# The first microseconds rearranged: tap diagonals on VectorE, a shorter first convolution on TensorE, and w_in loaded in three pieces

## The chip, the cores and the metric

The kernel runs on one core of a Trainium2 chip. The metric is device time in microseconds, from the launch to the end of the program. Four runs of the kernel before gave a median of 681.24 us, between 681.12 and 681.43. One execution was profiled; it took 681.22 us, of which the trace's span, from the first recorded instruction to the last, holds 679.5 us. The remaining 1.7 us lie around the span.

## What is computed

A lightweight causal convolution over tokens, 7 taps wide, with one softmaxed set of taps for each of 8 heads (24 channels a head, 192 in all), followed by a two-layer network with a leaky ReLU. There are 8 sequences of 4096 tokens, so 32768 rows in all.

```python
# x: (8, 4096, 192)   weight: (8, 7)
w = softmax(weight, axis=-1)                       # one row of taps a head
x_pad = concatenate([zeros(6 tokens), x], axis=1)
conv[b, s, h, g] = sum_k w[h, k] * x_pad[b, s + k, h, g]
# w_in: (192, 2048)   w_out: (2048, 192)
h = conv.reshape(32768, 192) @ w_in
out = maximum(0.01 * h, h) @ w_out                 # float32
```

## The kernel before

**Tiling.** Channels lie in three chunks (`NCH`) of 64 (`CH`). Two sequences share the 128 partitions: the tile `xt[:, c, token]` has chunk c of sequence 0 on partitions 0 to 63 and of sequence 1 on 64 to 127. Work goes by `groups`: the first two blocks of 512 tokens are cut into four half groups of 256 tokens, and 30 whole groups of 512 follow. For each group TensorE forms the first product (`mm1`, line 494, into `ph`), ScalarE applies the leaky ReLU to `g` (line 501), and TensorE forms the second product of the group before (lines 511 and 574, into `po` and `acc2`). VectorE convolves the next group's tokens, one instruction for each tap and chunk (lines 226 and 232), and transposes the result (line 596); SyncE stores it (line 612). Order on each engine is the order of the program text; tiles carry their own waits. SyncE's queue also issues the DMA transposes of x (lines 117 and 203), and GpSimd's queue issues all loads.

**The start.** The first group has no group before it under which VectorE could convolve, so TensorE convolves it: a diagonal matrix of 64 x 64 holds one tap of 64 channels, and matrix products with shifted windows of `xt` add up in PSUM. A tap is split into a bf16 high part and a low part (`p` = 0 and 1), so a chunk needs 2 x 7 diagonals, each used on both 64-row halves. The array runs as four tiles of 64 x 64. `pe_conv_jobs` makes a list of pairs of matmuls, one pair for each diagonal; a chunk with `cross=True` sends its output to the other half of the columns, so that a straight and a crossed list together use all four tiles. `run` interleaves lists. The program text calls a slot of such a list a place: up to four matmuls of 256 columns that use different tiles at the same time. Before, the order is 7 places of chunk 0 alone, 7 of chunk 0 with chunk 2, 7 of chunk 1 with chunk 2 and 7 of chunk 1 alone: 28 places, 84 matmuls.

The diagonals are products of a folded identity (`ident2`, 128 x 64, bf16) with the taps (`whm`, float32, copied out of PSUM at line 407). VectorE makes five of these tables with `diag_wide` (line 413), ScalarE the other ten single diagonals with `diag_each` (line 421). After its diagonals VectorE forms `wml`, `rsum` and its reciprocal, then copies the first piece of w_in into the layout that the row tiles need (`spread_down`, line 320, and `spread_up`, line 323), takes one half of chunk 2 out of PSUM (line 276), copies the transposed x of the second half group (line 199) and forms `wk`, the float32 taps for its own convolutions. ScalarE takes the other accumulators out (line 452).

w_in comes in two pieces of 8 blocks of 128 columns (`load_w_in`, line 314). GpSimd's queue issues: piece 0 (two loads), x of half group 1 (`x_rows`, line 148, two loads), piece 1 (two loads), x of half group 2 (two), w_out (line 346, two), x of half group 3 (`x_half`, line 152, six), then x of block 2 (line 99). A unit `u` of `mm1` for a half group takes two blocks of w_in; units 0 to 3 use piece 0, units 4 to 7 piece 1. Between the units of the first group TensorE convolves chunks 0 and 2 of the second half group in the cuts `CUTS` = 6, 5 and 3 places, while VectorE convolves its chunk 1 and spreads piece 1.

**The stores.** `evac_t` stores a group with four DMAs (line 612); one group, number 17 of 34, is stored in eight smaller ones.

## Time and profile before

| what | value | how to read it |
|---|---|---|
| median of four runs | 681.24 us | 681.12 to 681.43 |
| the profiled execution | 681.22 us | its span is 679.5 us |
| TensorE matmuls, weight loads | 99%, 66% of the span | ends of matmuls are modelled, so this is occupancy and not peak rate |
| VectorE, ScalarE, GpSimd | 71%, 76%, 22% | busy share of the span |
| first matmul of the convolution (line 257) | at 5.60 us | 28 places follow |
| first transpose of half group 1 (line 188) | at 8.79 us | 12 matmuls |
| first matmul of the first product (line 494) | at 9.25 us | 24 matmuls, units 0 and 1 |
| first leaky ReLU (line 501) | at 10.13 us | |
| group 17's eight stores (line 612) | issued from 356.78 us, 5.58 us in all | other groups: four stores, 2.80 us |
| bytes moved | 53.27 MB, mean 78 GB/s | DMA engines are busiest in the first 16 us |

Times are microseconds from the start of the span. PE is TensorE's matmul, PEld its weight loads, DVE is VectorE, ACT ScalarE, POOL GpSimd and SP SyncE; L494 is line 494. In a timeline row the columns are start, length, engine, line, operation, tiles, shape and count.

### The profile page before, as it was taken

The page shows a single profiled execution, that of the slowest core. Times are in us where ns is not written, and L with a number is a line of the kernel's source. Part 1 is how long each engine was busy: PE and PEld are TensorE (multiplying, and loading weights), DVE is VectorE, ACT ScalarE, POOL GpSimd, SP SyncE. Part 2 cuts the span into 40 slices and gives each one's busy share as a digit, 9 for nine tenths or more (in the row PEclk, how much of TensorE's full clock was granted, in tenths as well). Part 3 has the DMA queues.
Part 4 walks back from the last instruction along what each step waited for, and adds up shares of the span by engine and source line. Part 5 has one row for each costly group of instructions (what it writes and reads, how often), then busy time and mean ns, then how long its engine had stood idle before and what let it go on. Part 6 is the DMA issues. An engine that isn't in the chain of part 4 may idle for free.

```text
span 679.5 us, 27093 instructions
## 1 busy us (share of the span) xinstructions
PE 675.7 (99%) x12444; PEld 447.4 (66%) x12444; DVE 480.6 (71%) x811; ACT 518.8 (76%) x608; POOL 146.3 (22%) x205
## 2 busy tenths in 40 slices
PE   9999999999999999999999999999999999999998
PEld 6997666666666666666666666666666666666667
DVE  7989467766768666778667687667786676876612
ACT  7899777777777778777777877778777777777781
POOL 7455210222201222211222112222022220000000
PEclk9999999999999999999999999999999999999999
DMA  9899846656647657556556565567465573321123
GB/s 152 97 115 104 55 79 88 80 64 72 91 75 96 73 55 88 83 85 86 63 65 89 82 92 73 59 84 94 73 87 68 61 96 71 72 56 33 34 49 94
DMA packets 213890, 53.27 MB, mean 78 GB/s; under 512 B 209296, under 2 KB 213392, under 8 KB 213776
## 3 DMA queue, kind: packets, MB, share of 16 engines
q0 software_dynamic: 98752, 13.97, 30.3%
q1 hardware_dynamic: 115008, 37.57, 27.5%
q8 instruction: 97, 1.59, 1.0%
q14 instruction: 17, 0.14, 0.1%
q10 hardware_dynamic: 16, 0.00, 0.0%
HBM read 28.31 MB, written 25.17 MB: 79 GB/s over the span
## 4 chain that ended last, share of the span: by engine, by line
PE 99%; DVE 0%; issue 0%
PE ph L494 49%; PE acc L574 44%; PE po L511 5%; PE acc L257 1%; PE warm L358 1%; PE ptr L188 0%; PE ptr L179 0%; DVE o_sb L624 0%; PE warm L394 0%; PE wps L394 0%
## 5 line engine op out<-in xcount | busy, mean ns | idle before, releaser
L501 ACT ACTIVATE g<-ph 128x1024 bf16<-128x1024 f32 x512 | 496.6, 1021 | 140.2 <-PE ph L494 140.0
L232 DVE SCALAR_TENSOR_TENSOR yt<-xt,wk,yt 128x512 bf16<-128x512 bf16 (+1 forms) x582 | 380.6, 719 | 0.2
L494 PE MATMUL ph<-yt,w_in 64*64 64x512 bf16 (+2 forms) x6048 | 377.1, 369 | 0.0
L574 PE MATMUL acc<-g,w_out 64*64 64x512 bf16 x5568 | 339.9, 376 | 0.0
L494 PEld LDWEIGHTS <-w_in 64*64 64x64 bf16 (+1 forms) x6048 | 229.5, 131 | 102.9 <-issue 0.6
L574 PEld LDWEIGHTS <-w_out 64*64 64x64 bf16 x5568 | 178.6, 118 | 118.5
L99 POOL DMA_DIRECT2D x_bf<-in_x_dram x180 | 133.9, 775 | 408.8 <-DMA xt<-x_bf 406.7
L596 DVE STREAM_TRANSPOSE o_t<-acc 128x512 f32<-128x512 f32 x87 | 72.1, 866 | 182.7 <-PE acc L574 182.7
L511 PE MATMUL po<-w_out,g 64*128 64x192 bf16 (+1 forms) x640 | 36.8, 243 | 0.0
L511 PEld LDWEIGHTS <-g 64*128 64x128 bf16 (+1 forms) x640 | 32.5, 95 | 3.2 <-issue 0.4
L226 DVE TENSOR_SCALAR yt<-xt,wk 128x512 bf16<-128x512 bf16 (+1 forms) x97 | 29.1, 325 | 2.9 <-ACT g L501 2.2
L584 ACT COPY junk<-junk 128x1 f32<-128x1 f32 x58 | 11.2, 192 | 4.1
L624 DVE COPY o_sb<-po 128x192 f32<-128x192 f32 x8 | 2.8, 356 | 6.8 <-PE po L511 4.2
L257 PE MATMUL acc<-xt,diag 64*64 64x256 bf16 x140 | 5.4, 272 | 0.0
L624 ACT COPY o_sb<-po 128x192 f32<-128x192 f32 x16 | 5.1, 324 | 0.3
L257 PEld LDWEIGHTS <-diag 64*64 64x64 bf16 x140 | 4.3, 106 | 1.3 <-DVE diag L413 0.7
L358 PE MATMUL warm<-const-bfloat16-1.0 128*128 128x512 bf16 (+3 forms) x12 | 4.3, 513 | 0.8 <-PEq L736 0.8
L152 POOL DMA_DIRECT2D x_half<-in_x_dram x6 | 4.3, 732 | 1.2 <-DMA x_rows<-in_x_dram 0.9
L358 PEld LDWEIGHTS <-const-bfloat16-1.0 128*128 128x128 bf16 x12 | 1.5, 138 | 2.5 <-issue 2.5
L148 POOL DMA_DIRECT2D x_rows<-in_x_dram x4 | 2.9, 742 | 0.0
L413 DVE TENSOR_TENSOR diag<-ident,whm 128x448 bf16<-128x448 bf16 (+1 forms) x5 | 2.6, 579 | 0.0
L421 ACT ACTIVATE diag<-ident,whm 128x64 bf16<-128x64 bf16 x10 | 2.5, 339 | 0.0
(47 smaller groups left out, 24.4 us busy)
## 6 DMA issues: line engine op xcount, KB each, us to landing
out_dram<-o_t SPq DMA_DIRECT2D x112, 192.0 KB, 4.7
x_bf<-in_x_dram POOLq DMA_DIRECT2D x180, 64.0 KB, 3.1
out_dram<-o_sb SPq DMA_DIRECT2D x8, 192.0 KB, 3.4
xt<-x_bf SPq DMA_TRANSPOSE x90, 3.7
w_out<-in_moe_w_out_dram POOLq DMA_DIRECT2D x2, 384.0 KB, 8.2
out_dram<-o_t SPq DMA_DIRECT2D x8, 96.0 KB, 2.1
out_dram<-o_sb SPq DMA_DIRECT2D x8, 96.0 KB, 1.7
w_in<-in_moe_w_in_dram POOLq DMA_DIRECT2D x2, 256.0 KB, 4.7
```

Source lines behind the costliest of these rows:

```text
L99: ins = nc.gpsimd.dma_start(out=t[:, c, :, e, :], in_=src[2 * rp + e, :, :, c * CH : (c + 1) * CH],)
L226: lambda s=src, d=dst, c=c: nc.vector.tensor_scalar_mul(d, s, wk[:, c, 0:1])
L232: lambda s=src, d=dst, c=c, k=k: nc.vector.scalar_tensor_tensor(out=d, in0=s, scalar=wk[:, c, k : k + 1], in1=d, op0=mybir.AluOpType.mult, ...
L257: lambda k=k, p=p, a=a, ps=ps, to=to, acc=accs[e * apart]: nc.tensor.matmul(out=acc[to, :T], lhsT=diag[c][ps, p, k, :], rhs=xt[0][ps, c, a ...
L358: nc.tensor.matmul(out=wa[:, 0, 0:cols], lhsT=ones[:, 0:128], rhs=ones[:, 0:cols], start=True, stop=True,)
L494: nc.tensor.matmul(out=ph[m : m + M, e, i * T : (i + 1) * T], lhsT=w_in_of(f, e, c, m, m + M), rhs=y[ps, c, t0 : t0 + T], start=(c == chun ...
L501: act = nc.scalar.activation(out=g[blk][:, nf * u : nf * (u + 1), :, t0 : t0 + T], in_=ph.rearrange("p e (i t) -> p i e t", i=nf), func=my ...
L511: return nc.tensor.matmul(out=po[m], lhsT=g[b][ps, fc, e, s * 128 : (s + 1) * 128], rhs=w_out[ps, fc, :], start=start, stop=stop,)
L574: ins = nc.tensor.matmul(out=acc2[gi, r][e * CH : (e + 1) * CH, 0:T], lhsT=w_out_of(ps, fc, r), rhs=g[b][ps, fc, e, t0 : t0 + T], start=fi ...
L584: seal = nc.scalar.copy(out=junk, in_=junk)
L596: nc.vector.transpose(out=osb[gi, 0][:, 0 : T // GB, :, r], in_=acc2.pop((gi, r))[:, 0:T].rearrange("p (j k) -> p j k", k=GB),)
L624: ins = copy(out=o_sb[:, n % 2, :], in_=po.pop(n))
```

## The change

1. The taps are copied out of PSUM as bf16 with every tap twice (`taps`), and each table of diagonals is one VectorE product over pairs of elements. All six tables are made on VectorE; ScalarE's ten single diagonals go. `wml`, `rsum`, its reciprocal and `wk` stand between and behind the tables.
2. The first convolution runs chunks 0 and 2 together through 14 places. Chunk 1 then uses all four array tiles by itself: its 256 tokens are cut in halves of 128, a straight and a crossed one (`pe_conv_quads`), in 14 slots of four matmuls with 128 columns, which the text counts as 7 places. The crossed half accumulates in the PSUM tile `wps`, and three instructions take chunk 1 out in place of one.
3. w_in comes in three pieces of 4, 4 and 8 blocks, the second and third between x of half groups 1 and 2. The second is spread right after the copies of half group 1, the third after two of VectorE's taps in place of three.
4. The first unit of `mm1` runs chunk by chunk over both of its blocks, in place of block by block.
5. Group 17 is stored in four DMAs like the others.

```diff
-    def diag_wide(c, p, n):
-        nc.vector.tensor_mul(
-            diag[c][:, p, 0:n],
-            ident2[:, None, :].to_broadcast([128, n, CH]),
-            whm[:, c, p, 0:n, None].to_broadcast([128, n, CH]),
-        )
-
-    def diag_each(c, p, ks):
-        for k in ks:
-            nc.scalar.activation(
-                out=diag[c][:, p, k, :], in_=ident2,
-                func=mybir.ActivationFunctionType.Copy, scale=whm[:, c, p, k : k + 1],
-            )
+    taps = const_pool.tile([128, NCH, 2, K + 1, 2], BF16, name="taps")
+    nc.vector.tensor_copy(
+        out=taps, in_=wps_hm[..., None].to_broadcast([128, NCH, 2, K + 1, 2])
+    )
+    def diag_wide(c, p):
+        shape = [128, K, CH // 2, 2]
+        nc.vector.tensor_mul(
+            diag[c][:, p].rearrange("p k (m t) -> p k m t", t=2),
+            ident2.rearrange("p (m t) -> p m t", t=2)[:, None].to_broadcast(shape),
+            taps[:, c, p, 0:K, None, :].to_broadcast(shape),
+        )
...
+    def pe_conv_quads(grp, c, crossed):
+        blk, t0, T = grp
+        n = T // 2
+        acc = psum_o.tile([128, ST], FP32, name="acc", tag="po")
+        accs = [(acc, acc), (crossed[:, 0], crossed[:, 1])]
+        jobs = []
+        for p in range(2):
+            for k in range(K):
+                a = BASE + k + blk * ST + t0
+                four = []
+                for h in range(2):
+                    for e in range(2):
+                        ps = slice(e * CH, (e + 1) * CH)
+                        to = slice((e ^ h) * CH, ((e ^ h) + 1) * CH)
+                        four.append(
+                            lambda k=k, p=p, a=a + h * n, ps=ps, to=to, acc=accs[h][e]: nc.tensor.matmul(
+                                out=acc[to, :n], lhsT=diag[c][ps, p, k, :],
+                                rhs=xt[0][ps, c, a : a + n],
+                                start=(k == 0 and p == 0),
+                                stop=(k == K - 1 and p == 1),
+                            )
+                        )
+                jobs.append(four)
+        def evac(straight, *scale):
+            y = yt[blk][:, c, t0 : t0 + T]
+            straight(y[:, 0:n], acc[:, :n], rsum[:, c, :])
+            for e in range(2):
+                ps = slice(e * CH, (e + 1) * CH)
+                frm = slice((1 - e) * CH, (2 - e) * CH)
+                scale[e](y[ps, n:T], crossed[frm, e, :n], rsum[frm, c, :])
...
-    NPW = 2
+    PIECES = [(0, RUN), (RUN, 2 * RUN), (2 * RUN, NFC)]
...
-    for rows in (0, 128):
-        load_w_in(1, rows)
+    for n in range(1, len(PIECES)):
+        for rows in (0, 128):
+            load_w_in(n, rows)
     load_first(2)
...
-    for p in range(2):
-        diag_wide(0, p, K)
-    diag_wide(2, 0, K)
-    diag_wide(1, 1, VK)
-    diag_wide(2, 1, K)
-    diag_each(1, 1, range(VK, K))
-    diag_each(1, 0, range(K))
+    diag_wide(0, 0)
+    diag_wide(2, 0)
+    diag_wide(0, 1)
+    nc.vector.tensor_add(wml, wps_l, taps[:, :, 1, :, 0])
+    diag_wide(2, 1)
...
+    diag_wide(1, 0)
     nc.vector.reciprocal(rsum, rsum)
+    diag_wide(1, 1)
...
-    pe_1, evac_1 = pe_conv_jobs(groups[0], 1, (1, 0))
-    run(pe_0[:K])
-    run(pe_0[K:], pe_2[:K])
+    pe_1, evac_1 = pe_conv_quads(groups[0], 1, wps)
+    run(pe_0, pe_2)
     evac_0(act_scale)
-    run(pe_1[:K], pe_2[K:])
-    run(pe_1[K:])
-    evac_2(act_scale, nc.vector.tensor_scalar_mul)
-    evac_1(act_scale)
+    evac_2(nc.vector.tensor_scalar_mul, act_scale)
+    run(pe_1)
+    evac_1(act_scale, nc.vector.tensor_scalar_mul, act_scale)
     transpose_first(1)
     evac_first(1, nc.vector.tensor_copy, nc.vector.tensor_copy)
...
+    spread_down(1)
+    spread_up(1)
...
-        for n in range(nf * NCH):
-            i, c = n // NCH, chunks[n % NCH]
+        wide = not (blk or t0 or u)
+        order = [(i, c) for i in range(nf) for c in chunks]
+        if wide:
+            order = [(i, c) for c in chunks for i in range(nf)]
+        for i, c in order:
...
-            parts = 2 if gi == len(groups) // 2 else 1
-            for h, q in product(range(2), range(parts)):
+            for h in range(2):
...
-                    for job in conv_1[:3]:
+                    for job in conv_1[:2]:
                         job()
-                    spread_down(1)
-                    spread_up(1)
-                    for job in conv_1[3:]:
+                    spread_down(2)
+                    spread_up(2)
+                    for job in conv_1[2:]:
```

## The prediction

> **What bounds the kernel now.** I read the page's first part and the chain that ended last, then the same chain over the first 20 us.
>
> ```profile
> span 679.5 us, 27093 instructions
> ...
> PE 675.7 (99%) x12444; PEld 447.4 (66%) x12444; DVE 480.6 (71%) x811; ACT 518.8 (76%) x608; POOL 146.3 (22%) x205
> ...
> PE 99%; DVE 0%; issue 0%
> ```
>
> TensorE is the chain from end to end. Is any of it waiting? ScalarE's marker between two rounds (line 584) comes once at the same point of each whole group; the timeline around the middle has it at:
>
> ```profile
> 341.82 0.19 ACT L584 COPY junk<-junk 128x1 f32<-128x1 f32 x1
> ...
> 362.54 0.19 ACT L584 COPY junk<-junk 128x1 f32<-128x1 f32 x1
> ...
> 403.98 0.19 ACT L584 COPY junk<-junk 128x1 f32<-128x1 f32 x1
> ...
> 424.70 0.19 ACT L584 COPY junk<-junk 128x1 f32<-128x1 f32 x1
> ```
>
> That is 20.72 us a group (403.98 - 362.54 is twice that). A group has 384 matmuls, and the chain lists 24 of them in 1.29 us, 54 ns each: 384 x 54 ns = 20.7 us. Nothing stalls there, so only the start can give or take time. The chain there, as start, length, engine, tile:
>
> ```profile
> 5.67 3.19 PE acc L257 x80
> 8.86 0.46 PE ptr L188 x12
> 9.31 1.43 PE ph L494 x24
> 10.75 0.78 PE acc L257 x24
> ...
> 12.97 0.67 PE acc L257 x20
> 13.64 1.55 PE ph L494 x24
> 15.19 0.45 PE acc L257 x12
> ```
>
> The reader sees TensorE work without a gap from 5.67 us. From 0.78 us for 24 matmuls and 0.45 us for 12, three places of four cost 0.33 us, 0.11 us a place, and each change of shape about 0.12 us. Then 28 places should take 28 x 0.11 + 0.12 = 3.20 us; they take 3.19. So the diagonals do not hold the convolution up even now: an earlier diagonal gives nothing by itself, and only fewer places do.
>
> **Place count (part 2 of the change).** Chunks 0 and 2 take 14 places: 14 x 0.11 = 1.54 us. Chunk 1 takes 14 slots of four matmuls with 128 columns. No row has four tiles at 128 columns. These are the nearest:
>
> ```profile
> 6.50 0.13 PEld L257 LDWEIGHTS <-diag 64*64 64x64 bf16 x4
> ...
> 8.79 0.53 PE L188 MATMUL ptr<-ident,x_rows 128*64 128x128 bf16 x12
> ```
>
> The first is a 10 ns look at the weight loads: four of them, each 106 ns long (the tile's row gives 102/106/108), all lie inside 0.13 us. So the four tiles are loaded at the same time and their issue takes about 25 ns for four. The second is a run with 128 columns and two tiles: 0.46 us in the chain, less 0.12 for the change of shape, is 0.34 us for six pairs, 56 ns a pair, so one tile takes a new weight and 128 columns every 56 ns. If four tiles do what two do, a slot costs 56 ns and chunk 1 14 x 0.056 = 0.78 us. That is the low end. The high end is one matmul at a time at the smallest mean spacing in the trace, 0.34 us / 12 = 28 ns: 56 x 28 = 1.57 us. I take 0.78, by the weight-load row, which has this very tile shape. The convolution then takes 1.54 + 0.78 + 0.12 = 2.44 in place of 3.19: 0.75 us less; at the high end 0.04 more.
>
> The Trainium skill speaks against this part. "TensorE: Matmul & The Clock Gate", section "Wait — 56ns, not 53.3ns?", says that the starts of successive matmuls are never closer than about 25 ns, however few columns they have. By that figure, as an estimate, chunk 1 would take 56 x 25 ns = 1.4 us and the part would give 0.1 us. The page does not say whether it holds across array tiles, and the four loads above inside 0.13 us say that it need not.
>
> **Diagonals (part 1).** They remove ten ScalarE instructions (339 ns each, 2.49 us together, 5.33 to 7.82) and the five tables on VectorE. The rows of the stretch 4.4 to 9.9 us, grouped by shape:
>
> ```profile
> L413 DVE TENSOR_TENSOR diag<-ident,whm 128x448 bf16<-128x448 bf16 x4 | 2.3, 620 | 0.0
> ...
> L413 DVE TENSOR_TENSOR diag<-ident,whm 128x256 bf16<-128x256 bf16 x1 | 0.4, 418 | 0.0
> ```
>
> Slope (620 - 418) / 192 = 1.05 ns an element, fixed part 149 ns. Successive tables start 0.54 us apart (five in 2.56 us), 0.08 less than their length. The new table has bf16 on both sides in adjacent pairs. The nearest row of that kind is the sum of two bf16 halves of the identity (line 383): 64 elements in 174 ns, where 149 + 64 x 1.05 would be 216 and half the slope 183. So I take half the slope: 149 + 448 x 0.525 = 384 ns, 0.30 apart. The bounds are that and 620 ns, 0.54 apart. With VectorE starting at 4.47 (the copy of 96 in place of 48 elements adds 0.05), the tables end at 4.85 (0,0), 5.16 (2,0), 5.46 (0,1), 5.96 (2,1), 6.46 (1,0) and 6.96 (1,1), with 0.2 us for each small step between. TensorE needs them at 5.60, 5.60, 6.40, 6.40, 7.17 and 7.56: covered by at least 0.4 us, so they cost nothing.
>
> "VectorE: DVE Perf Modes", section "The perf-mode tier table (the rule you actually need)", gives a two-input product on bf16 twice the float32 rate; an estimate from that rule, half of 448 x 1.05 ns, makes a table 0.23 us shorter.
>
> **What then decides the first product (parts 2 and 4).** VectorE goes on: `wk` (0.20 + 0.20, moved here from behind the transposes), the spread of piece 0 at half its size (rows 423 and 824 ns for 1024 and 2048 elements, so 0.22 and 0.42) ending at 7.95, its half of chunk 2 (461 ns, line 276) ending at 8.45, its quarter of chunk 1 (461 - 128 x 1.05 = 327 ns) at 8.8. TensorE: transposes at 8.79 - 0.75 = 8.04, first product at 9.25 - 0.75 = 8.50. Chunk 0 and the spread are there by then, and chunk 2 is wanted two pairs later, at 8.74: covered by 0.25 us. Chunk 1 leaves PSUM in three instructions: its last accumulation ends near 8.15; ScalarE, behind its half of chunk 2 (0.47), needs two of about 0.38 us (rows 339 ns at 64 elements, 464 at 256) and is done between 8.85 and 9.11. Chunk by chunk the first product wants chunk 1 four pairs after its start, near 8.97; by blocks it would be two pairs, 8.74. So a wait of 0 to 0.2 us is left, I take 0.1, and part 4 is worth 0.2 at most. Behind that wait on TensorE stand the rest of units 0 and 1 and the first cut, and behind unit 0 ScalarE's first leaky ReLU; all of it is inside the sum.
>
> **w_in in pieces (part 3).** Two more issues on GpSimd's queue (585 ns each, 1.2 us) move x of half group 2, w_out, x of half group 3 and block 2 behind them. Their cover: x of half group 2 is wanted at 16.35 and landed 6.6 us after its issue at 6.8, at 13.4; w_out's halves landed near 15.1 and 17.1 and are wanted from 17.4 and from 19.4. With 1.2 us more, and wanted 0.65 sooner, they still land 1.1, 0.4 and 0.4 us ahead, so I cost it at nothing. Piece 1 must be spread by unit 2, near 10.8: loads of half the size, issued at the same 5.01, land about where x of half group 1 does now (3.60 + 4.6 to 4.3 + 4.4, so 8.2 to 8.7), and VectorE spreads them from about 9.5 to 10.3. Piece 2 must be ready for unit 4 at about 12.9. It has the bytes ahead of it that piece 1 has now (landing 5.01 + 5.0 and 5.55 + 5.5, so 11.1); two taps end at 11.1, the spread (0.54 + 0.97) at 12.6. Margin 0.3, before it was 0.35 (12.32 + 0.97 against 13.64). If its landing slips by the full 1.2 us the spread's second half runs from 12.3 and the wait is 0.4.
>
> **Stores (part 5).** Group 17's marker distance is 20.72 like all others; SyncE's queue gets 2.8 us shorter there, and TensorE never waited for it: nothing.
>
> **Sum.** Against the profiled execution (681.22, span 679.5, 1.7 around it): -0.75 for the places, +0.1 for chunk 1's wait, 0 for the rest, -0.65 in all. Steady groups merely shift. The median of the runs stands 0.02 above that execution, so 680.6 us.
>
> **Rivals.** (a) The four tiles take turns: chunk 1 costs 1.57 us, the start is 0.04 longer, chunk 1's wait is hidden under the later transposes; 681.2 to 681.3. For it: no row of the trace has a mean spacing under 27 ns. Against: the four loads inside 0.13 us. (b) Slower: the tables run at the full 1.05 ns. Then they end at 5.09, 5.63, 6.17, 6.92, 7.66 and 8.40; TensorE waits at the eighth place until 6.96 (0.5 us) and at chunk 1's second half until 8.44 (0.3), and VectorE's queue behind them ends the spread at 9.4, its half of chunk 2 at 9.9 and its quarter of chunk 1 at 10.25. Unit 0 then ends near 10.5 where it now ends near 9.93: +0.57 us, 681.8. It starts to cost when VectorE's chain is some 0.2 us longer than I put it, and the change becomes a loss at 0.9 (chunk 1's quarter at 9.7 in place of 8.8, two pairs and 0.04 us of signalling before 9.93). For it: one input repeats itself with no step, as it does now at full price. Against: line 383. (c) Piece 2 lands 1.2 us late: 0.4 of the gain goes, 681.0. (d) A gap at the start keeps TensorE slow for longer. In the chain three 128-column matmuls take 0.32 us at 4.60, 107 ns each, though the granted clock reads full there; after 8.79 that width costs 56. Time spent in the slow state costs half of itself; three more microseconds would be 1.5 us, 682.7. Against: the work before 5.60 is unchanged.
>
> **How the numbers follow.** What this kernel's measurement can tell from no change is about 0.2%, 1.36 us. Forecast 64%; (a) 12%; (b) 12%; (c) 6%; (d) 3%; 3% for a gain or loss that I do not see. All but (d) and the last stay within 1.36 us: within 0.2% 0.93, slower 0.05, faster 0.02 (even 7 places at no other cost are only 0.77 us). The range reaches from the places' full gain with 0.2 us to spare, 680.3, to (b), 681.8.
>
> **What would show it.** Right: 56 new matmuls in about 0.8 us, tables of about 384 ns, transposes at about 8.05, the first leaky ReLU at about 9.5, markers still 20.72 apart and about 0.65 us earlier. Wrong: new matmuls 28 ns apart, tables of 620 ns, a weight load of the first product waiting for VectorE, or any marker distance that differs.

## The result, and the profile after

The changed kernel takes 682.24 us (median of 33 runs, 680.93 to 683.46) where the kernel before, in the runs beside them, takes 681.44 us (53 runs, 681.05 to 682.08). The ratio is 1.0012, with a 95% interval of 1.0007 to 1.0017: 0.8 us slower, which is less than the 0.2% that were to count as a difference, but on the other side from the forecast of 680.6 us, and above its range. The profiled execution took 682.13 us.

The page's first part and the shares of the chain that ended last:

```profile
span 680.4 us, 27140 instructions
...
PE 675.7 (99%) x12472; PEld 447.3 (66%) x12472; DVE 481.4 (71%) x815; ACT 516.6 (76%) x599; POOL 147.2 (22%) x207
...
PE 97%; DMA 1%; POOL 1%; DVE 0%; issue 0%; POOLq 0%
```

The span is 0.9 us longer. TensorE has 28 matmuls more, as the four-tile chunk asks for, and the same busy time. New in the chain are the transfer engines and GpSimd with 1% each, some 7 us: the chain now goes back to a load. The markers on ScalarE (start, length, engine, line, operation) show where:

```profile
342.49 0.19 ACT L625 COPY junk<-junk 128x1 f32<-128x1 f32 x1
...
363.21 0.19 ACT L625 COPY junk<-junk 128x1 f32<-128x1 f32 x1
```

They are still 20.72 us apart, and 0.67 us later than before (341.82, 362.54). So the steady part did not change, and the start lost 0.67 us. The other 0.25 us of the longer span lie behind the landing of the last store; what fills them was not looked for. Here are TensorE's weight loads of the start, with the idle time of that queue and what ended it in brackets; 0.20 of it is usual at a change of shape.

```profile
8.21 0.36 PEld L186 LDWEIGHTS <-x_rows 128*64 128x64 bf16 x12
...
9.43 0.76 PEld L534 LDWEIGHTS <-w_in 64*128 64x128 bf16 x14 [0.28 <-issue]
10.39 0.58 PEld L255 LDWEIGHTS <-diag 64*64 64x64 bf16 x24 [0.19 <-issue]
...
13.28 0.11 PEld L534 LDWEIGHTS <-w_in 64*128 64x128 bf16 x1 [0.20 <-issue]
14.28 1.24 PEld L534 LDWEIGHTS <-w_in 64*128 64x128 bf16 x23 [0.89 <-DVE w_in L360]
```

The transposes of half group 1 start at 8.21 in place of 8.79: 0.58 us gained. The first product waits 0.28 us for chunk 1, so the first cut starts at 10.39 in place of 10.68: 0.29 gained. The kernel before has the first cut and unit 4 here:

```profile
10.68 0.58 PEld L257 LDWEIGHTS <-diag 64*64 64x64 bf16 x24 [0.20 <-issue]
...
13.57 1.35 PEld L494 LDWEIGHTS <-w_in 64*128 64x128 bf16 x24 [0.20 <-issue]
```

Unit 4 starts at 13.28, about 0.3 ahead of before (13.57), issues one weight load, and then stands for 0.89 us for a copy on VectorE, the spread of the last piece of w_in (line 360). The lead of 0.3 becomes, with that wait and some 0.1 us behind it, the lag of 0.67 that the markers show. The chain of waits names what that copy waited for:

```profile
6.65 6.72 DMA w_in<-in_moe_w_in_dram
...
13.40 0.84 DVE w_in L360
...
14.29 1.50 PE ph L534 x23
```

and VectorE's timeline shows the same from its own side:

```profile
11.58 0.49 DVE L230 SCALAR_TENSOR_TENSOR yt<-xt,wk,yt 128x256 bf16<-128x256 bf16 x1
12.77 0.42 DVE L357 COPY w_in<-w_in 64x1024 bf16<-64x1024 bf16 x1 [0.70 <-DMA w_in<-in_moe_w_in_dram]
13.40 0.83 DVE L360 COPY w_in<-w_in 64x2048 bf16<-64x2048 bf16 x1 [0.21 <-DMA w_in<-in_moe_w_in_dram]
14.26 1.01 DVE L230 SCALAR_TENSOR_TENSOR yt<-xt,wk,yt 128x256 bf16<-128x256 bf16 x2
```

VectorE finishes two taps of half group 1 and then waits, with the other taps queued behind it. Piece 2's two loads are there by 12.77 and 13.40, where the copies start. In the kernel before, the two loads of the last piece had landed by 11.1, ahead of its copies, which waited for nothing:

```profile
11.75 0.54 DVE L320 COPY w_in<-w_in 64x1024 bf16<-64x1024 bf16 x1
12.32 0.97 DVE L323 COPY w_in<-w_in 64x2048 bf16<-64x2048 bf16 x1
```

Two groups of the stretch 4.4 to 10.2 us (busy time and mean length of one behind the bar) say that the arithmetic did what was hoped:

```profile
L457 DVE TENSOR_TENSOR diag<-ident,taps 128x448 bf16<-128x448 bf16 x6 | 2.1, 381 | 0.0
...
L295 PEld LDWEIGHTS <-diag 64*64 64x64 bf16 x56 | 0.9, 106 | 0.0
```

A table takes 381 ns in place of 620, and the 56 weight loads of the four-tile chunk lie inside 0.9 us.

### The profile page after: what moved, and what is told of

Read it like the earlier page. It is cut to its first block, busy times and chain, and to the rows that moved or that the text cites. A ratio compares the mean times of both kernels' runs of the same rounds, so it can differ in the third digit from the quotient of the medians.

```text
span 680.4 us, 27140 instructions
## 1 busy us (share of the span) xinstructions
PE 675.7 (99%) x12472; PEld 447.3 (66%) x12472; DVE 481.4 (71%) x815; ACT 516.6 (76%) x599; POOL 147.2 (22%) x207
## 3 DMA queue, kind: packets, MB, share of 16 engines
q8 instruction: 97, 1.59, 1.0%
## 4 chain that ended last, share of the span: by engine, by line
PE 97%; DMA 1%; POOL 1%; DVE 0%; issue 0%; POOLq 0%
PE ph L534 48%; PE acc L615 44%; PE po L552 5%; DMA w_in<-in_moe_w_in_dram 1%; POOL w_in L351 0%; POOL x_rows L146 0%; DVE w_in L360 0%; POOL sel L334 0%; PE ptr L186 0%; PE acc L255 0%; DVE o_sb L663 0%; POOL ident masks.py:199 0%; POOL sel L332 0%; POOL ident masks.py:197 0%; POOLq masks.py:199 0%
## 5 line engine op out<-in xcount | busy, mean ns | idle before, releaser
L625 ACT COPY junk<-junk 128x1 f32<-128x1 f32 x58 | 11.1, 192 | 4.4 <-ACT g L542 0.4
L255 PE MATMUL acc<-xt,diag 64*64 64x256 bf16 x112 | 4.0, 279 | 0.0
L255 PEld LDWEIGHTS <-diag 64*64 64x64 bf16 x112 | 2.9, 110 | 1.4 <-DVE diag L457 0.7
L351 POOL DMA_DIRECT2D w_in<-in_moe_w_in_dram x6 | 3.4, 594 | 0.0
```

The costliest lines, as they stand in the source:

```text
L255: lambda k=k, p=p, a=a, ps=ps, to=to, acc=accs[e * apart]: nc.tensor.matmul(out=acc[to, :T], lhsT=diag[c][ps, p, k, :], rhs=xt[0][ps, c, a ...
L625: seal = nc.scalar.copy(out=junk, in_=junk)
```

## The experiments

Fifteen kernels ran, timed in several rounds beside the kernel before, whose median was between 681.38 and 681.62 from one call to the next. "The changed kernel" is the one of the diff.

**Two pieces in place of three.**

```diff
-    PIECES = [(0, RUN), (RUN, 2 * RUN), (2 * RUN, NFC)]
+    PIECES = [(0, NFC // 2), (NFC // 2, NFC)]
...
-    spread_down(1)
-    spread_up(1)
```

> The changed kernel with w_in in two pieces of eight blocks again, loaded and spread as before; all else stays changed. Theory L (the change loses because w_in's last piece lands late): unit 4 no longer waits for the spread, the median falls from 682.2 to between 680.9 and 681.6, and the runs lie within 1 us of each other in place of 2.5. The full first piece makes VectorE's spread 0.6 us longer, so chunk 1 is waited for longer and part of the gain goes. Rival V (the loss is VectorE's longer chain at the start, not the load): the median stays at 682 or rises.

Measured: 681.76 us (11 runs, 681.43 to 682.74), before 681.45; ratio 1.0005 (0.9996 to 1.0014). No wait for w_in is left, but TensorE's weight loads show another:

```profile
8.22 0.11 PEld L186 LDWEIGHTS <-x_rows 128*64 128x64 bf16 x1 [0.36 <-DMA x_rows<-in_x_dram]
9.24 0.36 PEld L186 LDWEIGHTS <-x_rows 128*64 128x64 bf16 x11 [0.91 <-DMA x_rows<-in_x_dram]
```

TensorE is ready for the transposes at 7.9 and gets x of half group 1 only at 9.2. In the kernel before, x landed at 8.71 and was wanted at 8.79. A shorter convolution alone runs straight into this load: with the loads of before there was next to nothing to gain. The time lies just above the range of theory L and below that of rival V, so by itself it settles neither.

**Three pieces alone, in the kernel before.**

```diff
-    NPW = 2
+    PIECES = [(0, RUN), (RUN, 2 * RUN), (2 * RUN, NFC)]
```

> The kernel before with w_in in three pieces and nothing else changed. Theory L: the last piece lands near 13.4 us, its spread ends near 14.3, unit 4 (due at 13.57) waits 0.7 us, median near 682.1 with runs over 2 us apart. Rival V: 681.2 to 681.5, runs within 1 us.

Measured: 681.62 us (11 runs, 681.26 to 682.04), ratio 1.0004 (0.9995 to 1.0013). Piece 2 is there by 12.28 and 12.98, its spread ends at 13.74, and unit 4 waits 0.22 us for it, although nothing else was changed:

```profile
13.79 0.48 PEld L501 LDWEIGHTS <-w_in 64*128 64x128 bf16 x10 [0.22 <-DVE w_in L326]
```

Theory L had a wait of 0.7 us, and the time lies between the ranges of the two theories: the late landing is shown here, a loss in time is not.

**Piece 0 spread by ScalarE.**

```diff
-    spread_down(0)
-    spread_up(0)
+    spread_down(0, nc.scalar.copy)
+    spread_up(0, nc.scalar.copy)
```

> The changed kernel with the first piece's two spread copies on ScalarE, which is idle from 5.4 to 7.5 us. Theory L: chunk 1's wait on TensorE (0.28 us) goes, but unit 4 still waits for the last piece at 13.4 us and its spread, so the time stays at 682.2 +- 0.2. Rival V: 0.3 to 0.9 us faster than the changed kernel, since VectorE's chain is 0.9 us shorter. Rival P (VectorE's wide copies hold up GpSimd's writing of DMA descriptors): the last piece lands 1 us or more earlier, near 12.3, and the time falls to 681.3.

Measured: 682.24 us (11 runs, 681.47 to 683.46), ratio 1.0014 (1.0005 to 1.0023). The wait for chunk 1 is shorter, not gone, and the first cut starts at 10.26, 0.13 earlier:

```profile
9.30 0.76 PEld L534 LDWEIGHTS <-w_in 64*128 64x128 bf16 x14 [0.20 <-issue]
```

From the transposes to the first cut it takes 2.08 us, where the changed kernel takes 2.18 and the kernel before 1.89. What is left is ScalarE's: four instructions in a row from 7.50 to 9.25. Nothing is gained in the time: piece 2's second half still came out at 13.26, behind a wait of 1.28 us, its spread ended at 13.95, and unit 4 started at 14.02. In this execution TensorE also stood in the second cut, for 0.87 us up to 13.36, for another reason (below), and would not have been ready before 14.02 either. So VectorE's load is not what the change loses by, but this execution does not price piece 2 alone.

**Two pieces, the first one small.**

```diff
+    PIECES = [(0, RUN), (RUN, NFC)]
```

> The changed kernel with two pieces of 4 and 12 blocks: the number of loads of before, with a small first load. It is slow by construction, since unit 2 waits for the second piece; what is read is its landing. If the number of loads on GpSimd's queue delays the last piece, it lands near 11.3 us like before's. If a small first load, which leaves the DMA engines without work while GpSimd issues the next, delays it, it lands near 12.5 to 13.4. The median should be near 682.5 to 684.

Measured: 686.21 us (2 runs, 685.06 and 687.36), ratio 1.0072. The twelve blocks are there by 11.40 and 12.59, 6.3 to 7.0 us after their issue, and unit 2 needs them:

```profile
11.41 0.11 PEld L534 LDWEIGHTS <-w_in 64*128 64x128 bf16 x1 [0.24 <-DMA w_in<-in_moe_w_in_dram]
13.60 2.27 PEld L534 LDWEIGHTS <-w_in 64*128 64x128 bf16 x23 [2.07 <-DVE w_in L360]
```

The wait is 2.07 us, but the time is 4.8 us above before: after the wait the same 23 weight loads take 2.27 us where they take 1.24 after short waits. The granted clock shows why (busy share of PE, PEld, DVE, ACT, POOL, then granted clock, DMA share, GB/s):

```profile
14.00:15.00 1.00, 1.00 (x13) 0.73 (x10) 0.93 (x3) 0.00 (x0) 1.00 (x2) 0.50 1.14 207
...
17.00:18.00 1.00, 1.00 (x27) 0.80 (x19) 0.00 (x0) 0.41 (x1) 0.31 (x1) 1.00 1.35 83
```

It is 0.50 from 13.44, within the wait, to 16.85, for 3.41 us. In the changed kernel, whose wait is 0.89 us, it stays at 1.00. So this idle stretch of 2 us cost its own length and some 1.6 us more: the 3.25 us at half clock that lie behind the wait, in which half of the work got done. One thing more bears on piece 2: the second load has no more issues ahead of it than in the kernel before, is issued at the same time (5.02 and 5.59; before 5.01 and 5.57), and up to its end as many bytes of w_in are moved, but its last half lands at 12.56 in place of 11.08. So the landing is 1.5 us later with a small piece in front, without any issue more; why was not settled.

**Half group 0 without piece 2.**

```diff
+        if first and f >= 2 * RUN:
+            f = RUN + f % RUN
```

> The changed kernel, in which units 4 to 7 of half group 0 multiply by piece 1's blocks in place of piece 2's; piece 2 is loaded and spread as before, but half group 0 no longer needs it. Theory L (the late landing of piece 2 is what the change loses): the wait of 0.7 us ahead of unit 4 goes, unit 4 starts near 13.6 us in place of 14.28, every later marker comes 0.6 to 0.7 us earlier, and the median falls from 682.24 to 681.5 to 681.7. Rival R (the loss comes from other waits or from the spread on VectorE that delays the taps behind it): the time stays at 682.1 to 682.3 with the wait gone or moved to the next half group.

Measured: 682.08 us (11 runs, 681.38 to 682.99), ratio 1.0011 (1.0002 to 1.0020). The wait at unit 4 is gone, and the time fell by 0.16 us where 0.6 was expected. VectorE's timeline and then TensorE's:

```profile
12.98 0.42 DVE L357 COPY w_in<-w_in 64x1024 bf16<-64x1024 bf16 x1 [1.63 <-DMA w_in<-in_moe_w_in_dram]
...
16.96 0.48 DVE L269 TENSOR_SCALAR yt<-acc,rsum 128x256 bf16<-128x256 f32 x1
```

```profile
18.52 0.59 PE L536 MATMUL ph<-yt,w_in 64*128 64x256 bf16 x7 [0.24 <-DVE yt L274]
```

The copy that nobody needs yet still stands in VectorE's queue until its load lands. Five taps and the evacuation of half group 1 come behind it: the evacuation starts at 16.96 (15.68 before), and half group 1's product waits for it. The late load costs by two roads, and this took away only one. (This kernel leaves out half group 0's product with piece 2: it multiplies by piece 1's blocks again.) Unit 4 is 0.21 us ahead of before, the first marker 0.55 behind; another 0.45 us go at 47.61, where TensorE waits for a tap of VectorE's that ends at 47.57.

**The two more issues alone, in the kernel before.**

```diff
+    pad = const_pool.tile([128, 2, CH], BF16, name="pad")
+    for n in range(2):
+        nc.gpsimd.dma_start(out=pad[:, n], in_=moe_w_in[0:128, n * CH : (n + 1) * CH])
     for rows in (0, 128):
         load_w_in(1, rows)
```

> The kernel before with two small loads (128 x 64 each) issued on GpSimd's queue just ahead of the second piece of w_in; nothing else changes. Theory I (what makes the last piece late is only the two more issues): this piece is issued 1.2 us later and lands 1.2 us later, near 11.2 and 12.3 in place of 10.0 and 11.1, its spread still ends by 13.4, and the time is that of before, 681.3 to 681.6. Rival S (the small pieces as such, half the bytes for each issue and each packet, cost most of the 2.3 us): the same landing as under I; if instead it lands at 12.8 to 13.4 as in the changed kernel, the two issues explain all of it, unit 4 waits 0.5 to 0.8 us and the time is 682.0.

Measured: 681.43 us (11 runs), before 681.41; ratio 1.0002 (0.9993 to 1.0010). The last piece lands 1.4 us later, at 12.45 in place of 11.08, and that still fits: its second copy waits 0.22 us for it and ends at 13.29, as before.

```profile
12.47 0.82 DVE L323 COPY w_in<-w_in 64x2048 bf16<-64x2048 bf16 x1 [0.22 <-DMA w_in<-in_moe_w_in_dram]
```

Of the 2.3 us by which piece 2 is late in the changed kernel, the two issues explain about 1.4.

**x of half group 1 on SyncE's queue**, with the changed kernel's three pieces, and the same with two pieces. Both take two issues off GpSimd's queue; ScalarE casts.

```diff
-        if q == 0:
+        if q < 2:
             x_nat[q] = stage_pool.tile([128, 2, HS, D], FP32, name="x_nat")
...
+    for s in range(HS):
+        nc.scalar.copy(out=x_rows[1][:, :, s], in_=x_nat[1][:, :, s])
```

> The changed kernel, with x of half group 1 loaded as float32 on SyncE's queue behind x of half group 0 and cast by ScalarE behind its two copies of the first transposes (two casts of some 0.5 us, done near 6.5); GpSimd issues two loads less ahead of pieces 1 and 2. Theory L: pieces 1 and 2 are issued 1.4 us earlier, piece 2 lands near 12.0 in place of 13.37, unit 4 waits 0 to 0.1 us, the median is 681.4 to 681.7, level with before. Rival B (the transfer engines and not the issues set the landing): piece 2 lands at 12.8 or later and the time stays at 682.0 to 682.3.

> As the run before it, but with w_in in two pieces of eight blocks, spread as in the kernel before (the second one behind the third tap). x of half group 1 no longer comes behind a large piece. Theory L: neither the transposes at 8.2 us nor unit 4 waits for a transfer; what stays is the spread of eight blocks on VectorE ahead of chunk 1 (0.4 + 0.8 us in place of 0.3 + 0.6), which makes the first product wait 0.5 us; the convolution's 0.6 us less that is a gain of 0.1 to 0.3 over the kernel before: 681.1 to 681.3. Rival R (the first 20 us give back what they are spared whatever the loads do): 681.5 to 681.8.

Measured: 681.54 us with three pieces (11 runs, 681.17 to 683.54; ratio 1.0005, 0.9996 to 1.0014), 682.33 with two (681.79 to 683.97; 1.0015, 1.0006 to 1.0023). The first fits the expectation in its median; in its profiled execution, the slowest of the eleven (683.54), x of half group 0 came at 5.20, so late that the first transposes waited 1.06 us, and the convolution ran at half pace (0.21 us a place, more on this below). That the new load got in the way of the one ahead of it is not shown: with the same loads on SyncE in the second kernel, x of half group 0 came at 3.89, as before. The second missed: the eight blocks of piece 0 landed at 8.61, VectorE waited 0.86 us there with chunk 2's evacuation queued behind, and the first leaky ReLU came at 10.98.

**Both roads to piece 2 closed**: the kernel of "half group 0 without piece 2", and the spread behind all seven taps.

```diff
-                    for job in conv_1[:2]:
+                    for job in conv_1:
                         job()
                     spread_down(2)
                     spread_up(2)
```

> The changed kernel, in which units 4 to 7 of half group 0 multiply by piece 1's blocks in place of piece 2's, as in the run that only did this, and piece 2 is spread behind all seven taps of half group 1's chunk 1 instead of behind the second. In that run VectorE stood 1.63 us in its queue for piece 2, and half group 1's evacuations came out 1.3 us late behind it. Theory L2 (the late piece costs twice: unit 4 waits for it, and VectorE's queue waits for it with the taps behind): now nothing waits for piece 2, the markers from 20 us on are 0.2 to 0.4 us ahead of the kernel before, and the median is 681.0 to 681.3. Rival R (the start gives the gain back in some way that has nothing to do with piece 2): 681.8 or more.

Measured: 681.49 us (11 runs, 681.16 to 682.46), before 681.62 in the same call; ratio 0.9999 (0.9990 to 1.0008). That is 0.6 us less than with one road closed, in medians of two calls whose intervals against before overlap a little, and level with before: the loss of the changed kernel is gone when nothing waits for piece 2. (Like the kernel that it is made from, it leaves out half group 0's product with piece 2.) The gain is not there in full, and the profiled execution (682.43) shows a place where it goes:

```profile
12.74 0.11 PEld L255 LDWEIGHTS <-diag 64*64 64x64 bf16 x3 [0.19 <-issue]
13.91 0.46 PEld L255 LDWEIGHTS <-diag 64*64 64x64 bf16 x17 [1.06 <-issue]
```

In the middle of the second cut, inside a place, where no change of shape makes a pause, TensorE stands for about 1.1 us, and no semaphore ends that wait. The run with ScalarE's spread had the same at 13.36.

**x of half group 1 on ScalarE's queue**, issued behind the reading of the taps and cast as in the two runs before, with three pieces; and then with four pieces of four blocks.

```diff
+            dma = nc.scalar.dma_start if q else nc.sync.dma_start
             for s in range(HS):
-                nc.sync.dma_start(out=x_nat[q][:, :, s], in_=rows[:, :, s])
+                dma(out=x_nat[q][:, :, s], in_=rows[:, :, s])
```

> The changed kernel with x of half group 1 loaded as float32 on ScalarE's queue, issued behind its reading of the taps (near 3.3 us) so that it can't come ahead of x of half group 0, and cast by ScalarE behind its copies of the first transposes. Nothing of the computation is left out. L2: pieces 1 and 2 are issued 1.4 us earlier, piece 2 lands at 11.5 to 12.2 in place of 13.37, VectorE and unit 4 wait at most 0.2 us for it, the median is 681.1 to 681.4. Rival B (the transfer engines are the limit, not the place of the issue): piece 2 lands at 12.8 or later, 681.9 to 682.3. A third way: the two casts hold up ScalarE's share of the convolution's evacuation, the transposes start late, and the first leaky ReLU comes after 10.2.

> As the run before it, with the last piece cut in two (four pieces of four blocks), the third spread behind two taps and the fourth behind four. L2: the third piece, due at unit 4, is half as long and lands 0.5 to 1 us earlier than piece 2 of the run before it, the fourth is due only at unit 6; no wait is left on either, 681.0 to 681.3, and level with the run before it if that one has no wait. Rival: the two more issues and their smaller packets eat it, 681.4 or more.

Measured: 681.77 us with three pieces (11 runs; ratio 1.0000, 0.9991 to 1.0009) and 681.58 with four (0.9997, 0.9988 to 1.0006), before 681.62. With three pieces, piece 2 was issued 1.4 us earlier and landed 1.0 us earlier, at 12.38; with four pieces no spread from piece 1 on waits for its load, and unit 4 starts at 13.81. Both computations are whole, and both are level with before, where the changed kernel is not. Neither reached the 681.0 to 681.4 that was expected. What they still have is the stop without a releaser, 0.88 and 0.62 us.

**What the stop is.** From the traces, for each execution: when TensorE's 449th recorded instruction and the one behind it start, and when the first 16 KB packet of the queue for instructions starts and ends on the transfer engines (us).

```
                          193rd   449th   450th    gap   packet         450th - packet's end
before                     7.83   14.05   14.15   0.11   11.26 - 12.21  1.94
three pieces alone         7.72   14.27   14.44   0.17   12.24 - 13.21  1.22
changed kernel             7.50   12.62   12.62   0.00    9.73 - 10.71  1.91
piece 0 by ScalarE         7.47   12.49   13.36   0.87   11.04 - 11.99  1.37
without piece 2            7.11   12.24   12.70   0.46   10.41 - 11.42  1.28
both roads closed          7.74   12.75   13.92   1.16   11.53 - 12.50  1.42
x1 by ScalarE, 3 pieces    7.08   12.60   13.48   0.88   11.11 - 12.06  1.42
x1 by ScalarE, 4 pieces    7.04   12.52   13.15   0.62   10.90 - 11.86  1.29
```

In five kernels the stop is behind the same instruction, and it ends 1.28 to 1.42 us after the packet is through; in no execution of this study does TensorE pass it less than 1.2 us after. The queue's bytes fit TensorE's instructions: the kernel before moves 97 such packets, 1.59 MB, which is 64 bytes for each of its 24888 matmuls and weight loads, so a packet holds 256 of them, and 449 is 193 and 256. I conclude that TensorE is waiting for its own instructions. That is argued from these rows; no run moved the packet alone. My first theory was that the change makes them due earlier by the 56 instructions that it adds. Four kernels were to test that.

**More instructions, and fewer.** 30 tiny warm-up matmuls for two long ones in the kernel before; and the four-piece kernel with 16 instructions less ahead of the second cut.

```diff
-    warm(6, ST)
+    warm(4, ST)
+    for _ in range(30):
+        nc.tensor.matmul(out=wa[0:CH, 0, 0:1], lhsT=ones[:, 0:CH], rhs=ones[:, 0:1], start=True, stop=True)
```

> The kernel before, in which the six long warm-up matmuls at the very start are four, and 30 tiny ones (64 x 1 column) stand in place of the other two: 28 matmuls and 28 weight loads more on TensorE's queue, as many as the four-tile chunk of the change adds, at a place where TensorE only waits for the taps. The computation and all loads are those of before. In five runs TensorE stood still behind its 449th recorded instruction, with no wait shown, until 1.3 to 1.4 us after a 16 KB instruction packet had left the transfer engines. Theory F (the change needs these instructions 56 places earlier, and their fetch is late): here the 449th instruction is a matmul near the start of the second cut, near 12.9 us in place of 14.1; the packet leaves near 12.2 as in before, so TensorE stands still behind that instruction until about 13.5, 0.4 to 0.7 us, and the median is 681.9 to 682.2. Rival G (the fetch is started earlier by as many instructions as it is needed earlier, and only the loads of the changed kernel make it late): no stall, 681.3 to 681.6.

```diff
+                if q == 1:
+                    nc.tensor.transpose(
+                        out=t[:, s, c, :],
+                        in_=x_half[q][:, c, s, :, :].rearrange("p e k -> p (e k)"),
+                        identity=ident,
+                    )
...
-    warm(3, 128)
+    warm(1, 384)
```

> The changed kernel with x of half group 1 on ScalarE's queue and w_in in four pieces, as in the run that had both, and with 16 instructions less on TensorE ahead of the second cut: ScalarE casts x of half group 1 into the layout of half group 0, so that its transposes are 6 of 128 x 128 in place of 12 of 128 x 64, and one warm-up matmul of 384 columns stands for three of 128. The computation is whole. Theory F: the 449th instruction comes 8 matmuls later, behind the 11th of the second cut and 0.3 us later, so the stall of 0.33 us seen there shrinks to 0 to 0.2; markers 0.3 to 0.5 us ahead of the kernel before, median 681.0 to 681.4. Rival G: the fetch comes as much later as it is needed later, the stall stays at 0.3, 681.5 to 681.8.

Measured: the tiny matmuls took 1.76 us, the convolution behind them began 0.95 us later and took 4.3 us in place of 3.2 (its first eleven four-tile places took 0.21 us each; full clock is on record only from 8.97), and the time is 683.74 us (7 runs; ratio 1.0029): no stop, but also nothing that speaks on the question. The kernel with 16 fewer takes 681.21 us (11 runs, 680.84 to 682.55), before 681.46: ratio 0.9997 (0.9988 to 1.0006), the lowest median of the study and not to be told from before. It had no stop in the second cut, but its packet was also early (9.80 to 10.78). Its first leaky ReLU is at 9.49 (10.13 before) and its first marker between rounds at 20.11 (20.59). Of the 0.64 us at the leaky ReLU 0.14 are an earlier start of the convolution (5.46, before 5.60) and not the shorter one. It then loses 0.3 of the 0.48 us at one place:

```profile
45.82 0.19 PEld L544 LDWEIGHTS <-w_in 64*128 64x128 bf16 x3
46.41 0.79 PEld L544 LDWEIGHTS <-w_in 64*128 64x128 bf16 x9 [0.40 <-issue]
```

An instruction packet had left the transfer engines at 45.06, 1.35 us before 46.41, but this stop is another one: it is not at a packet's boundary (instruction 1834 is no multiple of 256 behind the 449th), and the chain shows what ended it, a tap of VectorE's:

```profile
43.71 2.66 DVE yt L238 x4
46.37 0.04 issue
46.41 1.27 PE ph L544 x10
```

In the kernel before, VectorE's tap there ended at 46.11 and TensorE's products began at 46.33.

**Warm-up cut into short matmuls.** As many columns, 46 instructions more, in the kernel before and in the four-piece kernel.

```diff
-    warm(6, ST)
+    warm(24, 128)
...
-    warm(1, ST)
-    warm(1, 384)
+    warm(4, 128)
+    warm(3, 128)
```

> The kernel before, in which warm-up matmuls of 512 and 384 columns are cut into matmuls of 128 columns: the same columns (128 of them took 107 ns there, 512 took 427), but 23 matmuls and 23 weight loads more on TensorE's queue ahead of everything, near the 56 instructions that the change adds. Loads, engines and computation are those of before; the start shouldn't move, unlike in the run with 30 tiny matmuls, whose start came 0.95 us later and which therefore says nothing of this. Theory F: the 449th recorded instruction is now one that TensorE reaches near 13.05 us in place of 14.1; the instruction packet leaves near 12.2, TensorE goes on 1.35 us after it, near 13.55, so it stands still 0.3 to 0.7 us behind that instruction and the median is 681.8 to 682.2. Rival G (the fetch is started as much earlier as it is due earlier): no stall, 681.3 to 681.6.

> The changed kernel with x of half group 1 on ScalarE's queue and w_in in four pieces, with the same warm-up matmuls cut into 128 columns: 46 instructions more ahead. Without them TensorE stood still 0.33 us behind the 449th instruction in the profiled execution and the median was 681.58. Theory F: the 449th instruction is reached near 11.2 us in place of 12.5, in the third unit's product; with the packet leaving near 11.9 the stall is 1.3 to 1.9 us and the median 682.5 to 683.2; if the fetch is started earlier by part of that, 0.6 to 1.3 us and 682.0 to 682.5. Rival G: 681.4 to 681.7, stall as before.

Measured: 681.38 us in the kernel before (11 runs, 681.04 to 682.93; ratio 1.0005, 0.9996 to 1.0014) and 681.66 in the other (1.0004, 0.9995 to 1.0013). No stop in either. The 449th instruction came at 13.01 and 11.51, 1.0 us earlier in both, and the packets at 10.10 and 8.73, 1.2 and 2.2 us earlier. My first theory fell: a mere count of instructions moves the packet as well. What fits all rows is the time between the request and the need. If the request is made some 256 instructions of 64 bytes, one packet, ahead (a guess from the packet's size), the kernel before takes 6.2 us from the 193rd to the 449th, and the changed kernel 5.1, since a slot of the four-tile chunk issues eight instructions in the 56 ns in which a place of one list issued four, or of two lists eight, in 0.11 us. From the 193rd to the packet's start 2.0 to 4.5 us pass in these executions; with 0.95 us for the packet and 1.35 behind it, 6.2 us holds up to 3.9 of them, and 5.1 only up to 2.8. That the request is made there was not tried.

## Why the prediction was wrong

The sum was -0.65 us against the profiled execution; its markers show +0.67. The difference of 1.32 us has three terms.

- **The loads, 0.97 us: the step that failed.** "Piece 2 must be ready for unit 4 at about 12.9. It has the bytes ahead of it that piece 1 has now (landing 5.01 + 5.0 and 5.55 + 5.5, so 11.1)", and "so I cost it at nothing". It landed at 13.38, 2.3 us later. The step moved issues on GpSimd's queue for every load behind w_in, but for piece 2 itself it counted bytes, as if the transfer engines stayed as full as they were before. They did not. One row of the windows for the kernel before and one for the changed kernel (busy share of PE, PEld, DVE, ACT, POOL, then granted clock, DMA share, GB/s):

```profile
8.00:9.00 1.00, 1.00 (x24) 0.80 (x22) 1.00 (x2) 0.75 (x3) 1.00 (x3) 1.00 1.02 184
```

```profile
8.00:9.00 1.00, 1.00 (x38) 0.82 (x30) 0.95 (x3) 0.84 (x3) 1.00 (x2) 1.00 0.70 94
```

  GpSimd is busy throughout with issues of 0.5 to 0.75 us each, and the smaller pieces behind them leave the engines at 0.70 and 94 GB/s where they were at 1.02 and 184 in this row. The two issues alone explain 1.4 us of the 2.3 (measured in the kernel before); 0.9 us is a longer way from issue to landing, 6.7 us where the loads behind two small issues took 5.8, and its cause is not settled. Piece 1 points the same way: the prediction had it at 8.2 to 8.7, but with the issue times of before and half the bytes it landed at 9.80 and 10.32, hardly ahead of the whole piece before (9.98 and 11.08), and with nothing more ahead of it. Of the 0.97 us, 0.89 are the wait at unit 4. Rival (c) had the mechanism, at 1.2 us late and 0.4 lost: mis-sized, and with one road only. The second road, VectorE's queue standing at the copy with half group 1's taps behind it, was in none of the cases: the prediction named what stands behind TensorE's wait, and not what stands behind VectorE's. The run with one road closed gives its price: 0.6 us of median between it and the run with both closed, with the intervals given there.
- **The places, 0.17 us.** They gave 0.58 and not 0.75. The four-tile chunk is as predicted, 14 slots of 56 ns. The first two places of chunks 0 and 2 took 0.215 and 0.187 us in this execution, where 0.11 was expected and the later ones took it. The trace's record of the granted clock begins at 5.98 us, with full clock; up to there the matmuls go at half that pace, and the 1.00 in a row ahead of it stands for no record. The prediction's "the granted clock reads full there", in rival (d), is that misreading: its slow matmuls at 4.60 lie ahead of 5.54, where the record of the kernel before begins. In the other executions the record begins between 3.50 and 10.02 us, and where that falls within the convolution the doubling of the pace goes with it. Four kernels that do the same up to the convolution have it at 3.97, 5.92, 5.98 and 6.47. So this term seems to be chance of the execution and not a wrong price: where full clock came before the convolution, as with 16 instructions fewer (4.73), the way to the transposes took the predicted 2.44 us, 5.46 to 7.91. The first line is that kernel's, the second the changed kernel's:

```profile
5.46 1.46 PEld L263 LDWEIGHTS <-diag 64*64 64x64 bf16 x55 [0.16 <-issue]
```

```profile
5.61 1.61 PEld L255 LDWEIGHTS <-diag 64*64 64x64 bf16 x56 [0.73 <-DVE diag L457]
```

  What sets the moment was not tried. It moves single executions by some tenths of a microsecond, and that much stands in any comparison of two profiled executions at the start.
- **Chunk 1's wait, 0.18 us.** 0.28 and not 0.1. VectorE spread piece 0 in 0.29 + 0.60 us, put at 0.22 + 0.42; its evacuations came later by that, and ScalarE's last one behind them. Taking the spread off VectorE took away 0.1 of the wait; the rest is ScalarE's four instructions in a row, and the time did not change, as a later wait was still there.

What was right: the tables at 381 ns (384 put), the four tiles side by side, so that rival (a) and rival (b) fall; the stores, at nothing; the steady part, untouched. The range failed because the loads stood in it as a term of zero, with 6% and 0.4 us for their being late.

The Trainium skill's "TensorE: Matmul & The Clock Gate", section "Wait — 56ns, not 53.3ns?", says that starts of matmuls are not closer than about 25 ns. Here the four of a slot start within 4 ns, and 56 of them take 0.8 us, 14 ns each; the sum by that page would have put the part at 0.1 us. So the floor does not hold between array tiles; whether it holds for one tile no run here shows.

So what would the idea be worth? With the loads out of the way, 0.58 less 0.28 is 0.3 us at the start, of 681, in this execution, and 0.75 less 0.28, some 0.5 us, where full clock comes before the convolution. The best kernel of the study is 0.25 us below before in its median, with an interval from 0.9988 to 1.0006. The first convolution was not a bound that stood alone: x of half group 1 (wanted 0.08 us after it landed), w_in for unit 4 (0.3 us), TensorE's own instructions (0.6 us, from 1.94 less 1.35, if the stop is theirs) and VectorE's taps at 46 us (0.2 us) all stood just behind it.

## What to carry to other kernels

Before a stage on the bound engine is made shorter, list what each following instruction waits for and by how much it is early; the gain is no larger than the smallest of these margins. A load cut in pieces can be late by its place in the issuing queue though fewer bytes stand ahead of it (1.4 of 2.3 us here, the rest open), and it costs twice when an in-order engine has a copy of it in the middle of other work. Idle time on TensorE that ends with no releaser may be its instruction fetch: look for a 16 KB packet on the instruction queue some 1.3 us before it ends, and first whether another engine's result came just before, as at 46.41. Before two executions are compared at the start, compare the pace of the same matmuls.

## What I had not expected of the hardware

- TensorE can stop without a releaser at the start, perhaps for its own instructions (argued above, not shown): 0.46 to 1.16 us inside a place, at the 449th recorded instruction in five kernels, each ending 1.28 to 1.42 us after an instruction packet was through.
- After an idle 2.07 us, 23 weight loads took 2.27 us in place of 1.24, with the granted clock at 0.50 for 3.41 us; after 0.89 us they took 1.24 at 1.00.
- The granted clock is on record only from some moment between 3.50 and 10.02 us, and up to it the matmuls run at half pace (places of 0.21 us, 0.11 behind it).
- 30 matmuls of one column took 1.76 us at the start, 59 ns each, nearly as long as four of 512 columns (1.86 us).
